# Attention and two gated feed-forward layers on one core: another layout of q and k in the attention's transposes and scores

## The chip, the cores and the metric

One core of a Trainium2 chip. The metric is the device time of one execution in microseconds; three runs of the kernel before gave 864.93, 865.22 and 866.91 us.

## What is computed

q, k and v have the shape (4, 8, 576, 64): batch, heads, tokens, head dimension; p has 32 rows per head instead of 576. All are float32.

```
def sm_attn(qq, kk, vv):
    s = scale * np.matmul(qq, kk.transpose(0, 1, 3, 2))
    s = s - np.max(s, axis=-1, keepdims=True)
    a = np.exp(s)
    a = a / (np.sum(a, axis=-1, keepdims=True) + 1e-09)
    return np.matmul(a, vv)
p_packed = sm_attn(p, k, v)
out = sm_attn(q, p_packed, p_packed)
x = out as 2304 tokens x 512
x = softplus(x @ w_in) @ w_out          # 512 -> 2048 -> 512
y = (sigmoid(x @ w_gate) * (x @ w_val)) @ w_out2    # 512 -> 1536 -> 512
```

## The kernel before

The work has three parts: the attention, the first feed-forward layer (lines 551 to 691) and the second (from line 701). The program is unrolled, and attention and first layer are woven into each other: `attn_unit` (line 380) is a generator, one unit is half of a batch's heads (4 heads, 8 units u = 0 to 7), and each `yield` ends a stage. `att_tick` (line 534) moves one unit on by a stage; the loop at line 880 calls it between the products of the first layer, through `between` (line 685), at a pace that has the units of a batch done when that batch's first layer begins. `jobs` holds the preparations of weights (three VectorE instructions per block of weight in `convert`, line 165). The order within each engine is then fixed when the program is built, by data readiness in a model of the engines; on the chip each engine takes its own queue in order.

Loads go out on SP's queue. `load_kqv` (line 218) reads a unit's k, q and v, each of 4 heads x 576 tokens x 64, into slots (areas of the tile `xa`, or the tile `acc6`), as 96 rows (partitions) of 6 tokens per head, 1,536 bytes in one piece. A slot is filled again when `done_kqv` has said that its last reader has been issued, and the transfer waits for that reader.

A unit's stages, as far as they matter here:

- p is transposed (line 384), and two ScalarE copies (line 387) put it in `pT`, a tile with zeros elsewhere, so that two heads stand in one product.
- `tr_pair` (line 357) turns k: for each pair of heads POOL copies the six chunks into the order chunk, head, dimension (`by_chunk`, line 348), TensorE transposes six blocks of 96x128 (line 362), and ScalarE evicts two banks of 288 columns (line 369). q goes the same way in later stages.
- Scores of p (line 400): four products of 288 columns over the full 128x128 array, two passes each, so eight instructions. Their 128 output rows are 4 heads x 32 rows of p, and each row has its 576 tokens in two banks (`s1`).
- The softmax over 576: maximum over both banks (line 408), one exponential with its sum (line 411), reciprocal, and the normalisation (line 420).
- The result a1 is transposed (line 434, evicted at line 435) and multiplied by v (line 453, 64 output columns in alternating halves of the array), which gives `pp`. Two ScalarE copies (line 463 calls line 96) put it in `bdT`, which the first layer's products of weights also read (lines 583 and 603). For units 0 to 2 `warm` (line 373) issues 12 instructions without a use of their result.
- Scores of q (line 478): 12 products, 24 instructions, of qT by `bdT`, and the softmax over 32 (lines 488 to 497; the last normalisation is POOL's), in two halves of 12x32 columns.
- Two stages later the result is transposed (line 506) and split into `A2h` and `A2l`, which the first layer reads (lines 113 to 115).

Lines 113 to 115 and 674 to 677 are the large products of the layers; line 587 and lines 610 to 620 handle the product of p's values and w_in.

## Time and profile before

| | us |
|---|---|
| median of three runs | 865.22 (864.93 to 866.91) |
| the profiled execution | 869.49 |
| its span in the trace | 867.7 |
| TensorE busy | 846.9 |
| VectorE busy | 587.9 |
| POOL busy | 475.8 |
| ScalarE busy | 339.8 |

The rows further down use short names: PE is TensorE's products and PEld its loads of the stationary side (beside PE), DVE VectorE, ACT ScalarE, POOL GpSimd, SP SyncE; a q behind a name is that engine's sequencer, and L362 is line 362 of the kernel before. An arrow <- names what is read, or what ended a wait. A line of code can be that of a helper that many call. Products are pipelined and the end of each is modelled, so distances between starts tell more than durations do. A granted clock of 1.00 is TensorE's full 2.4 GHz, 0.50 its lower level of 1.2 GHz.

### The profile page before, as it was taken

The numbers are of one execution on the slowest core, as the hardware profiler recorded it, in microseconds if no ns is written. First come the engines' busy times: TensorE is split into PE (matmuls) and PEld (weight loads), VectorE is DVE, ScalarE is ACT, GpSimd is POOL, SyncE is SP. The second block draws the span as 40 slices with busy tenths as digits, with TensorE's granted clock in tenths as the row PEclk, the third lists the DMA queues.
The fourth block names the chain that finished last, engine by engine and source line by source line (L and its number), as shares of the span: only waits on it lengthen the run. The fifth ranks groups of instructions, "written<-read, shape, count | busy, mean of one in ns | idle before, by whom it ended". The sixth has DMA issues, their size and how long they took to land.

```text
span 867.7 us, 15523 instructions
## 1 busy us (share of the span) xinstructions
PE 846.9 (98%) x6112; PEld 794.4 (92%) x6112; DVE 587.9 (68%) x1004; ACT 339.8 (39%) x626; POOL 475.8 (55%) x453
## 2 busy tenths in 40 slices
PE   7899999999999999999899999999999999999997
PEld 5789989999999999999889999999988999999996
DVE  1785566956365646646788687887897746667665
ACT  4367665554433434444433332222352432322210
POOL 4364333245655545575669786876984634436400
PEclk9899999999999999999999999999999999999999
DMA  9974321203033402400054655744515413213003
GB/s 227 209 207 117 83 56 29 74 25 99 1 98 92 135 12 87 127 26 1 1 177 146 188 152 149 207 132 128 163 51 151 115 47 90 67 43 110 13 1 109
DMA packets 58023, 85.53 MB, mean 99 GB/s; under 512 B 6368, under 2 KB 39264, under 8 KB 57952
## 3 DMA queue, kind: packets, MB, share of 16 engines
q1 hardware_dynamic: 56944, 83.31, 34.3%
q10 hardware_dynamic: 1008, 1.25, 0.4%
q8 instruction: 48, 0.79, 0.4%
q14 instruction: 23, 0.19, 0.1%
HBM read 65.67 MB, written 18.87 MB: 97 GB/s over the span
## 4 chain that ended last, share of the span: by engine, by line
PE 83%; DVE 8%; DMA 3%; ACT 2%; POOL 2%; issue 2%; SPq 0%; POOLq 0%; ACTq 0%; DVEq 0%
PE bank L115 8%; PE bank L113 8%; PE bank L114 8%; PE ps L674 7%; PE ps L675 7%; PE ps L677 7%; PE ps L1022 5%; PE ps L1023 5%; PE ps L1024 5%; PE ps L113 4%; PE ps L115 4%; PE ps L114 4%; PE ps L603 2%; PE ps L478 2%; PE ps L362 1%
## 5 line engine op out<-in xcount | busy, mean ns | idle before, releaser
L113 PE MATMUL bank<-aop,BH 128*128 128x288 f32 x672 | 199.2, 296 | 3.0 <-DVE work L987 1.1
L115 PE MATMUL bank<-aop,BL 128*128 128x288 f32 x672 | 198.9, 296 | 0.0
L114 PE MATMUL bank<-aop,BH 128*128 128x288 f32 x672 | 198.0, 295 | 0.2 <-DVE aop L101 0.2
L682 DVE TENSOR_TENSOR xa<-xa,ps 128x288 f32<-128x288 f32 x224 | 100.3, 451 | 105.8 <-PE ps L677 105.4
L101 POOL TENSOR_TENSOR ghl<-g,ghl 128x576 fp32r<-128x576 f32 x64 | 93.3, 1458 | 134.7 <-ACT ghl L108 125.2
L674 PE MATMUL ps<-ghl,woh 128*128 128x288 f32 x512 | 149.6, 307 | 2.6 <-DVE xa L682 2.4
L675 PE MATMUL ps<-ghl,wol 128*128 128x288 f32 x512 | 144.4, 297 | 0.0
L113 PEld LDWEIGHTS bank<-aop,BH 128*128 128x128 f32 x672 | 126.3, 188 | 8.7 <-issue 2.1
L114 PEld LDWEIGHTS bank<-aop,BH 128*128 128x128 f32 x672 | 126.6, 188 | 4.1 <-DVE aop L101 0.4
L115 PEld LDWEIGHTS bank<-aop,BL 128*128 128x128 f32 x672 | 126.6, 188 | 0.2 <-POOL BL L101 0.2
L101 POOL TENSOR_TENSOR BL<-cv,BH 128x512 fp32r<-128x512 f32 (+1 forms) x96 | 118.2, 1246 | 3.6 <-ACT BH L108 2.4
L677 PE MATMUL ps<-ghl,woh 128*128 128x288 f32 x512 | 109.5, 295 | 0.0
L674 PEld LDWEIGHTS ps<-ghl,woh 128*128 128x128 f32 x512 | 97.0, 189 | 5.1 <-ACT aop L737 2.1
L675 PEld LDWEIGHTS ps<-ghl,wol 128*128 128x128 f32 x512 | 97.2, 190 | 0.6
L975 DVE TENSOR_TENSOR work<-work,bank 128x576 f32<-128x576 f32 (+1 forms) x100 | 70.8, 724 | 30.7 <-PE bank L115 29.8
L1022 PE MATMUL ps<-oh,gv 128*128 128x512 f32 x216 | 84.5, 391 | 1.0 <-DVE xa L1030 0.5
L1023 PE MATMUL ps<-ol,gv 128*128 128x512 f32 x216 | 85.0, 393 | 0.0
L1024 PE MATMUL ps<-oh,gv 128*128 128x512 f32 x216 | 84.9, 394 | 0.0
L677 PEld LDWEIGHTS ps<-ghl,woh 128*128 128x128 f32 x512 | 82.7, 189 | 0.0
L1030 DVE TENSOR_TENSOR xa<-xa,ps 128x512 f32<-128x512 f32 x90 | 61.5, 684 | 28.8 <-PE ps L1024 28.4
L113 PE MATMUL ps<-A2h,wph 128*128 128x288 f32 x256 | 77.6, 303 | 0.3 <-ACT wph L587 0.3
L115 PE MATMUL ps<-A2h,wpl 128*128 128x288 f32 x256 | 76.3, 298 | 0.4 <-DVE wpl L101 0.4
(131 smaller groups left out, 1594.5 us busy)
## 6 DMA issues: line engine op xcount, KB each, us to landing
cv<-B SPq DMA_DIRECT2D x52, 256.0 KB, 2.7
B<-cv SPq DMA_DIRECT2D x48, 256.0 KB, 4.0
raw_in<-in_moe_w_in_dram SPq DMA_DIRECT2D x16, 512.0 KB, 3.9
raw_out<-in_moe_w_out_dram SPq DMA_DIRECT2D x16, 512.0 KB, 3.6
raw_g<-in_moe_w_gate_dram SPq DMA_DIRECT2D x12, 512.0 KB, 4.1
raw_v<-in_moe_w_val_dram SPq DMA_DIRECT2D x12, 512.0 KB, 4.5
raw_o<-in_moe_w_out_dram SPq DMA_DIRECT2D x12, 512.0 KB, 4.1
xa<-in_q_dram SPq DMA_DIRECT2D x6, 576.0 KB, 6.9
```

The lines of the kernel that those rows point to most:

```text
L101: eng.tensor_tensor(lo, x, hi.bitcast(F32), op=ALU.subtract)
L113: nc.tensor.matmul(ps, wh, xh, start=first, stop=False)
L114: nc.tensor.matmul(ps, wh, xl, start=False, stop=False)
L115: nc.tensor.matmul(ps, wl, xh, start=False, stop=last)
L674: nc.tensor.matmul(out_, wh[:, ms], gh[:, f], start=f == 0, stop=False)
L675: nc.tensor.matmul(out_, wl[:, ms], gh[:, f], start=False, stop=False)
L677: nc.tensor.matmul(out_, wo_hl[c, f][0][:, ms], gl[:, f], start=False, stop=f == 1)
L682: nc.vector.tensor_tensor(dst, dst, out_, op=ALU.add)
L975: nc.vector.tensor_tensor(to, x, y, op=ALU.add)
L1022: nc.tensor.matmul(bank, gh[:, ts_], oh, start=f == 0, stop=False)
L1023: nc.tensor.matmul(bank, gh[:, ts_], ol, start=False, stop=False)
L1024: nc.tensor.matmul(bank, gl[:, ts_], oh, start=False, stop=f == 1)
```

## The change

k and q are read as 128 rows, one for each of 4 heads x 32 groups of 18 tokens; a row is 4,608 bytes in one piece. Each block of 128 columns holds two neighbouring tokens, so a transposed block has the even token's 64 dimensions in partitions 0 to 63 and the odd one's in 64 to 127. `turn` makes three such transposes and one eviction, which puts the columns in the order that a1 and v need; POOL's copies by chunk are gone. v is read as before. k0 still comes in two transfers, cut by columns and no longer by heads.

The scores of p are, for each head, one product whose stationary side `pt_` holds p twice, once for each half, so that its 64 output rows are 2 parities x 32 rows of p; two heads fill the 128 rows of a bank, in alternating halves of the array. A row of p now has its 576 tokens in two rows of the same bank. The maximum of the two is found by a product with `swap` (which exchanges the halves) and a minimum of the negated values, their sum by a product with `both`. There is one exponential and one normalisation for each bank.

The scores of q read p's values from `bdq`, filled by four more copies (two on ScalarE, two on VectorE), and come in groups of 16x32 and 8x32 columns.

```
@@ load_kqv @@
             if tag == 6:
-                t = att.tile([CT, KQV], F32, tag="acc6", name=f"{nm}{u}")
+                t = att.tile([P, KQV], F32, tag="acc6", name=f"{nm}{u}")
             else:
-                t = xa[:CT, KQV * tag : KQV * (tag + 1)]
+                t = xa[:, KQV * tag : KQV * (tag + 1)]
             src = {"k": k, "q": q, "v": v}[nm][b, 4 * g : 4 * g + 4]
-            if nm == "v" and u >= VCH:
...
-            else:
-                t = t.rearrange("p (h c d) -> p h c d", h=4, c=NC)
-                n = 2 if (nm, u) == ("k", 0) else 4
-                for hh in range(0, 4, n):
-                    nc.sync.dma_start(
-                        t[:, hh : hh + n], src[hh : hh + n].rearrange("h (r c) d -> r h c d", c=NC)
-                    )
+            if nm == "v":
+                t = t[:CT].rearrange("p (h c d) -> p h c d", h=4, c=NC)
+                nc.sync.dma_start(t, src.rearrange("h (r c) d -> r h c d", c=NC))
+            else:
+                t = t[:, : 9 * P]
+                src = src.rearrange("h (r c) d -> (h r) (c d)", r=NK)
+                cut = 3 * P if (nm, u) == ("k", 0) else 0
+                for x in (slice(0, cut), slice(cut, 9 * P)):
+                    if x.start < x.stop:
+                        nc.sync.dma_start(t[:, x], src[:, x])
@@ constants @@
-    pT = [att.tile([P, 4 * P], F32, name=f"pT{i}") for i in range(2)]
-    for t in pT:
+    swap, both = (att.tile([P, 2, 2, NK], F32, name=y) for y in ("swap", "both"))
+    idv = ident.rearrange("p (e i n) -> p e i n", e=2, i=2)
+    for i in range(2):
+        nc.gpsimd.tensor_scalar(swap[:, :, i], idv[:, :, 1 - i], 1.0, 0.0, op0=ALU.mult, op1=ALU.add)
+    nc.gpsimd.tensor_tensor(both, swap, idv, op=ALU.add)
+    swap, both = (x.rearrange("p e i n -> p (e i n)") for x in (swap, both))
+
+    pT, bdq = (
+        [att.tile([P, 4, 2, NK], F32, name=f"{y}{i}") for i in range(2)] for y in ("pT", "bdq")
+    )
+    for t in pT + bdq:
         nc.gpsimd.memset(t, 0.0)
@@ by_chunk and tr_pair go, turn comes @@
+    def turn(src, n, dst):
+        ps = bank1()[:, : 3 * P]
+        for c in range(3):
+            o = (3 * n + c) * P
+            nc.tensor.transpose(ps[:, c * P : (c + 1) * P], src[:, o : o + P], ident)
+        nc.scalar.activation(
+            dst.rearrange("p h (m r x) -> p x m h r", m=3, x=3)[:, n],
+            ps.rearrange("p (m h r) -> p m h r", m=3, h=4), AF.Copy,
         )
@@ attn_unit @@
-        kT = att.tile([P, 2, S], F32, tag="kT", bufs=1, name="kT")
-        tr_pair(kt, 0, kT, nc.scalar)
-        yield
-        tr_pair(kt, 1, kT, E1)
+        kT = att.tile([P, 4, HS], F32, tag="kT", bufs=1, name="kT")
+        for n in range(3):
+            turn(kt, n, kT)
+            if n == 1:
+                yield
...
         s1 = bank2()
-        for hf in range(2):
-            for j in range(2):
+        for j in range(2):
+            for e in range(2):
                 nc.tensor.matmul(
-                    s1[:, hf, :HS],
-                    pT[u % 2][:, P * j : P * j + P],
-                    kT[:, j, hf * HS : (hf + 1) * HS],
-                    start=j == 0,
-                    stop=j == 1,
+                    s1[64 * e : 64 * e + 64, j, :HS],
+                    pt_[:, 2 * j + e].rearrange("p i n -> p (i n)"), kT[:, 2 * j + e],
+                    start=True, stop=True,
                 )
-        mx = att.tile([P, 4], F32, tag="mx", bufs=2, name="mx")
-        nc.vector.tensor_reduce(mx[:, 0:1], s1[:, :, :HS], op=ALU.max, axis=AX.XY)
...
+        mx = att.tile([P, 10], F32, tag="mx", bufs=2, name="mx")
+        nc.vector.tensor_reduce(mx[:, 0:2], s1[:, :, :HS], op=ALU.max, axis=AX.X)
+        nc.vector.tensor_scalar(mx[:, 2:4], mx[:, 0:2], -SC, None, op0=ALU.mult)
+        other = s1[:, 1, 508:510]
+        nc.tensor.matmul(other, swap, mx[:, 2:4], start=True, stop=True)
+        nc.vector.tensor_tensor(mx[:, 4:6], mx[:, 2:4], other, op=ALU.min)
+        a1 = att.tile([P, 2, HS], F32, tag="a1", bufs=1, name="a1")
+        for j in range(2):
+            nc.scalar.activation(
+                a1[:, j], s1[:, j, :HS], AF.Exp,
+                bias=mx[:, 4 + j : 5 + j], scale=SC, accum_out=mx[:, 6 + j : 7 + j],
+            )
+        total = s1[:, 1, 510:512]
+        nc.tensor.matmul(total, both, mx[:, 6:8], start=True, stop=True)
+        nc.vector.tensor_scalar(mx[:, 8:10], total, 1e-9, None, op0=ALU.add)
+        nc.vector.reciprocal(mx[:, 8:10], mx[:, 8:10])
+        for j in range(2):
+            nc.vector.tensor_scalar(
+                a1[:, j], a1[:, j], mx[:, 8 + j : 9 + j], None, op0=ALU.mult
+            )
...
         done_kqv("v", u)
         warm(u, pp[:, 3 * P :], 6)
+        for i in range(2):
+            for e in range(2):
+                copy(
+                    e == i, bq[64 * i : 64 * i + 64, e::2, i],
+                    heads(pp[64 * e : 64 * e + 64], 32 * e, 64),
+                )
...
-        for hf in range(2):
+        for ms in ((0, 1), (2,)):
             s2 = bank1()
-            for c in range(3):
+            w = 2 * P * len(ms)
+            for m in ms:
                 for j in range(2):
...
+                    for e in range(2):
+                        o = (m - ms[0]) * 2 * P + 64 * (odd ^ j) + 32 * e
+                        nc.tensor.matmul(
+                            s2[:CT].rearrange("p (c x) -> p c x", x=P)[
+                                :, 2 * (m - ms[0]) : 2 * (m - ms[0]) + 2, o % P : o % P + NK
+                            ],
+                            qT[:, 2 * j + e, m * CT : (m + 1) * CT],
+                            bq[:, 2 * j + e],
+                            start=True,
+                            stop=True,
+                        )
...
-            (nc.gpsimd if (u, hf) in PMU or u >= PMA else nc.vector).tensor_tensor(
-                a2, a2, m2[:, 1].unsqueeze(2).to_broadcast([CT, 12, NK]), op=ALU.mult
+            nc.gpsimd.tensor_tensor(
+                a2, a2, m2[:, 1].unsqueeze(2).to_broadcast([CT, n, NK]), op=ALU.mult
             )
```

## Rows read from the trace of the kernel before

**Rows 1.** The page, part 1: busy us (share of the span) xinstructions, TensorE's line.
```profile
PE 846.9 (98%) x6112; PEld 794.4 (92%) x6112; DVE 587.9 (68%) x1004; ACT 339.8 (39%) x626; POOL 475.8 (55%) x453
```
**Rows 2.** Windows: busy us (xinstructions) by engine, granted clock, DMA share, GB/s.
```profile
42.00:62.00 20.00, 19.04 (x190) 15.86 (x186) 18.06 (x33) 15.48 (x39) 11.78 (x11) 1.00 0.68 185
```
**Rows 3.** Waits of TensorE, 40 to 175 us: us in total, times, longest.
```profile
PE ps L506 <- POOL a L496: 1.0, 2, 0.7
```
**Rows 4.** Chain of waits at the start: start us, us, what.
```profile
6.26 10.95 DMA xa<-in_q_dram
...
17.39 0.84 POOL x L351
...
18.27 0.72 PE ps L362 x6
```
**Rows 5.** Windows before and in the fall of the granted clock.
```profile
16.50:18.50 2.00, 0.23 (x3) 0.23 (x4) 0.43 (x2) 0.48 (x2) 1.11 (x2) 1.00 1.11 229
18.50:25.50 7.00, 7.00 (x75) 6.71 (x74) 4.10 (x9) 2.88 (x8) 0.61 (x2) 0.56 0.97 252
```
**Rows 6.** Windows while q and v are read, and while a weight is read.
```profile
15.00:17.00 2.00, 1.48 (x11) 1.03 (x9) 0.94 (x3) 0.71 (x2) 0.00 (x0) 1.00 1.09 242
...
20.20:21.20 1.00, 1.00 (x14) 0.78 (x12) 0.00 (x0) 1.00 (x4) 0.00 (x0) 0.50 1.11 352
```
**Rows 7.** Chain of waits, steady part: TensorE's groups.
```profile
80.96 1.88 PE ps L583 x16
...
88.52 0.66 PE ps L434 x6
89.17 1.94 PE ps L400 x8
...
97.28 2.01 PE ps L478 x24
99.29 0.50 PE ps L362 x6
```
**Rows 8.** Timeline of TensorE after line 583: start us, us, what.
```profile
82.77 0.40 PE L113 MATMUL ps<-A2h,wph 128*128 128x288 f32 x1
83.01 0.29 PE L114 MATMUL ps<-A2l,wph 128*128 128x288 f32 x1
83.14 0.29 PE L674 MATMUL ps<-ghl,woh 128*128 128x288 f32 x1
```
**Rows 9.** Groups by line and form, 0 to 300 us: busy us, mean ns | idle before.
```profile
L351 POOL TENSOR_SCALAR x<-xa 96x768 f32<-96x768 f32 x22 | 19.2, 883 | 25.7 <-DMA xa<-in_k_dram 7.7 <-PE ps L362 5.9 <-issue 5.0
...
L369 ACT ACTIVATE kT<-ps 128x288 f32<-128x288 f32 x32 | 11.6, 409 | 4.7 <-PE ps L400 3.5 <-PE ps L362 0.6
...
L435 ACT ACTIVATE a1T<-ps 96x384 f32<-96x384 f32 x16 | 7.0, 483 | 0.7 <-PE ps L434 0.6
...
L185 DVE SCALAR_TENSOR_TENSOR w_in<-raw_in,w_in 128x512 int32<-128x512 int32 x6 | 5.7, 949 | 0.1
...
L96 ACT ACTIVATE bdT<-ps 64x64 f32<-64x64 f32 x16 | 3.5, 216 | 10.7 <-PE ps L378 7.1 <-PE ps L453 3.5
...
L411 ACT ACTIVATION_READ_ACCUMULATOR a<-ps,mx 128x1 f32 x8 | 1.6, 201 | 0.0
...
L409 DVE TENSOR_SCALAR mx<-mx 128x1 f32<-128x1 f32 x8 | 1.2, 144 | 0.1
```
**Rows 10.** One slot's way: timelines of SP, POOL, TensorE, and that load's landing.
```profile
114.59 0.31 SPq L237 DMA_DIRECT2D k<-in_k_dram  x1
...
113.73 0.83 POOL L351 TENSOR_SCALAR x<-q 96x768 f32<-96x768 f32 x1 [0.78 <-PE ps L362]
...
118.96 1.33 PE L362 MATMUL ps<-ident,x 96*128 96x96 f32 x12
...
121.97 0.73 PE L362 MATMUL ps<-ident,x 96*128 96x96 f32 x6
...
DMA to landing us min/median/max: 4.7/4.7/4.7
```

More of the change, by code (lines that the diff above doesn't have):

```diff
@@ L421, in attn_unit @@
+        for j in range(2):
+            nc.vector.tensor_scalar(
+                a1[:, j], a1[:, j], mx[:, 8 + j : 9 + j], None, op0=ALU.mult
+            )
         yield
         qt = kqv.pop(("q", u))
-        qT = att.tile([P, 2, S], F32, tag="qT", bufs=2, name="qT")
-        tr_pair(qt, 0, qT, nc.scalar)
-        yield
-        tr_pair(qt, 1, qT, E1)
+        qT = att.tile([P, 4, HS], F32, tag="qT", bufs=2, name="qT")
+        for n in range(3):
+            turn(qt, n, qT)
+            if n == 1:
+                yield
@@ L427, in attn_unit @@
         done_kqv("q", u)
         yield
-        a1T = att.tile([CT, NC, P], F32, tag="a1T", bufs=2, name="a1T")
-        for hf in range(2):
+        a1T = att.tile([CT, 2, 3, P], F32, tag="a1T", bufs=2, name="a1T")
+        for j in range(2):
             pa = bank1()
-            for c in range(3):
-                o = (3 * hf + c) * CT
-                nc.tensor.transpose(pa[:CT, c * P : (c + 1) * P], a1[:, o : o + CT], ident)
+            for m in range(3):
+                nc.tensor.transpose(
+                    pa[:CT, m * P : (m + 1) * P], a1[:, j, m * CT : (m + 1) * CT], ident
+                )
@@ L443, in attn_unit @@
             for c in range(NC):
-                if u >= VCH:
-                    nc.tensor.matmul(
-                        pp[:, 64 * j : 64 * j + 64],
-                        vt[:, c, 2 * j : 2 * j + 2].rearrange("p h d -> p (h d)"),
-                        a1T[:, c, 64 * j : 64 * j + 64], start=c == 0, stop=c == NC - 1,
-                    )
-                    continue
+                m, i = divmod(c, 2)
                 for e in range(2):
-                    n0 = 64 * j + 32 * e
+                    o = 64 * e + 32 * i
                     nc.tensor.matmul(
@@ L455, in attn_unit @@
                         vt[:, 2 * j + e, c, :],
-                        a1T[:, c, n0 : n0 + 32],
+                        a1T[:, j, m, o : o + 32],
                         start=c == 0,
@@ L461, in attn_unit @@
         warm(u, pp[:, 3 * P :], 6)
+        for i in range(2):
+            for e in range(2):
[3 more added lines that the diff above has]
+                )
         for e in range(2):
@@ L470, in attn_unit @@
         a2s = []
-        for hf in range(2):
+        for ms in ((0, 1), (2,)):
             s2 = bank1()
-            for c in range(3):
+            w = 2 * P * len(ms)
+            for m in ms:
                 for j in range(2):
-                    slot = odd ^ j
-                    o = c * P + 64 * slot
-                    t = (3 * hf + c) * CT
-                    nc.tensor.matmul(
-                        s2[:CT, o : o + 64],
-                        qT[:, j, t : t + CT],
-                        bdT[:, 4 * half + 2 * g + j, 64 * slot : 64 * slot + 64],
-                        start=True,
-                        stop=True,
-                    )
-            s2v = s2[:CT, : 3 * P].rearrange("p (x n) -> p x n", n=NK)
-            m2 = att.tile([CT, 2, 12], F32, tag="m2", bufs=4, name="m2")
-            a2 = att.tile([CT, 12, NK], F32, tag="a2", bufs=4, name="a2")
+                    for e in range(2):
[8 more added lines that the diff above has]
+                            stop=True,
+                        )
+            n = w // NK
+            s2v = s2[:CT, :w].rearrange("p (x n) -> p x n", n=NK)
+            m2 = att.tile([CT, 2, 16], F32, tag="m2", bufs=4, name="m2")[:, :, :n]
+            a2 = att.tile([CT, 16, NK], F32, tag="a2", bufs=4, name="a2")[:, :n]
             nc.vector.tensor_reduce(m2[:, 0], s2v, op=ALU.max, axis=AX.X)
             nc.vector.tensor_tensor(
-                a2, s2v, m2[:, 0].unsqueeze(2).to_broadcast([CT, 12, NK]), op=ALU.subtract
+                a2, s2v, m2[:, 0].unsqueeze(2).to_broadcast([CT, n, NK]), op=ALU.subtract
             )
@@ L495, in attn_unit @@
             nc.vector.reciprocal(m2[:, 1], m2[:, 1])
-            (nc.gpsimd if (u, hf) in PMU or u >= PMA else nc.vector).tensor_tensor(
-                a2, a2, m2[:, 1].unsqueeze(2).to_broadcast([CT, 12, NK]), op=ALU.mult
+            nc.gpsimd.tensor_tensor(
+                a2, a2, m2[:, 1].unsqueeze(2).to_broadcast([CT, n, NK]), op=ALU.mult
             )
-            a2s.append(a2.rearrange("p x n -> p (x n)"))
+            a2s += [a2.rearrange("p x n -> p (x n)")[:, o : o + P] for o in range(0, w, P)]
         yield
```

46 lines of the change are left out of this document (5 added, 41 removed).

## The prediction

> **What bounds the kernel now.** I read the page first: TensorE is busy for 98% of the span [rows 1], so time is won where TensorE has less to do, or where it stands still. The part under change is the attention, which ends near 157 us of the span. In windows of 20 us one stretch of it stands out, from 42 to 62 us, where another engine comes near the end of its time: VectorE works 18.06 of 20 us, TensorE 19.04 [rows 2]. The view of TensorE's waits says how little it stands there: from 40 to 175 us the largest entry is 1.0 us behind POOL's normalisation [rows 3]. So from 40 us on a change is worth what it takes from, or gives to, TensorE's own queue.
>
> The chain of waits shows the other place, the start. The load of unit 1's q is issued at 6.26 us and lands 10.95 us later; POOL then copies it by chunk (0.84 us), and TensorE's transposes of it begin at 18.27 us [rows 4]. From there to 32 us the chain is TensorE without a break. TensorE's clock belongs to this: in the 2 us before 18.5 the engine was busy for 0.23 us, and in the 7 us from 18.5 it had a granted clock of 0.56, mostly its lower level [rows 5].
>
> **The loads at the start.** Between 15 and 17 us the transfers are q and v, 96 rows each, and move 242 GB/s; around 20.7 us it is a weight of 128 rows, and they move 352 GB/s, both with the DMA share full [rows 6]. A k or q is 589,824 bytes: 2.44 us at the first rate, 1.68 at the second. With 128 rows of 4,608 bytes the second is the nearest row, so each load is 0.76 us shorter. Four of them (k0, k1, q0, q1) lie ahead of 18.27 us: -3.05 us. The POOL copy between landing and transposes goes too: 18.27 - 17.39 = 0.88 us [rows 4]. Together -3.9 us. Next late is unit 0's normalised a1, whose softmax gets longer (below); I take half a microsecond off for it: **-3.4 us**, ends 0 and -3.9. The number of issues on SP's queue is the same, in the same order. POOL's new start work (swap, both, four half-size memsets in place of two) lies beside loads that last to 17 us: nothing; without that cover it is under one POOL instruction of 0.83 us.
>
> **POOL.** Four copies a unit go, 883 ns each [rows 9], 28 us over eight units. POOL is not the bound, so only the 1.0 us that TensorE waited for a normalisation behind such copies can come back [rows 3]: -0.5 us, ends 0 and -1.0.
>
> **Transposes and their evictions.** Before: 24 transposes a unit of 96 columns, 6 in 0.50 us, 2.0 us. After: 18 of 128 columns, 6 in 0.66 us, 1.98 us [rows 7]: nothing. ScalarE evicted eight times 409 ns and now six times 384 columns, 483 ns by the row of that size [rows 9]: -0.37 us a unit. No row writes every third element; below I bound it by 409 ns, above by twice 483, 966, and take 483, the row of the same length. ScalarE has slack (15.48 of 20 us in rows 2), so this stays off the path.
>
> **Scores of p.** Now eight instructions of 288 columns over the full array, 1.94 us [rows 7]. After, the same eight with 64 output columns, alternating between the halves. The same form exists in this kernel: line 583 puts 64 columns in alternating halves, and 16 instructions of 256 columns take 1.88 us, 117 ns each, less than half of what the full form takes for its length [rows 7]. At 288 columns that is 132 ns, eight make 1.06 us: -0.88 us a unit. Units 0 and 1 make their scores while TensorE waits for loads; for the other six **-5.3 us**.
>
> **The two small products.** swap and both add four instructions a unit (two passes each), with a stationary side of 128 columns and 2 moving ones. No row has 2 columns. Line 478 loads 96 columns for 64 moving ones, 24 in 2.01 us, 84 ns each; the transposes of 128 columns take 110 ns [rows 7]. The ends are 0 (the loads hide under a neighbour) and 110; I take 110, as all 128 columns must be loaded: 0.44 us a unit, **+2.6 us** for six. The Trainium skill, TensorEngine Tiling (Array Packing), section Instruction Overhead, says that a matmul has some 60 cycles of overhead and that one of free size 1 lasts as long as one of 60. By that alone four would be an estimated 0.1 us a unit and the sum 2 us lower; the 84 ns of line 478 speaks against it. Besides, products of another kind start late: after line 583 the second product comes 0.24 us after the first, where 0.13 is usual [rows 8]. Each small product is an island of its own kind: two such gaps a unit, 0.22 us, **+1.3 us**, ends 0 and 2.6.
>
> **The waits that come with them.** TensorE takes its queue in order. The first product waits for VectorE's maximum, the second for ScalarE's two sums, and everything behind them on TensorE, the other stages' products too, waits along. The queue is built so that other products lie between; the waits that exist are small [rows 3]. Ends: 0, and one long VectorE instruction ahead, 0.95 us [rows 9], at each of 12 products, 11.4 us. I take 0.1 each, nearest to how the present waits come out: **+1.2 us**.
>
> **VectorE and ScalarE.** VectorE gets a minimum (144 ns), a second normalisation (about 0.1 more for the same elements) and two copies of 64x64 (about 0.2 each): 0.65 us a unit. ScalarE: the split exponential costs one more reading of the sum (201 ns) and some 0.1 of fixed cost, two more copies 216 ns each, less 0.37: +0.4 us [rows 9]. After 62 us TensorE's own queue covers this, as its short waits say [rows 3]. Between 42 and 62 us, with VectorE nearly full, two units add 1.3 us there [rows 2]; I take **+0.5 us** on the path, ends 0 and 1.3. The second softmax handles the same elements in pieces of 512 and 256; its scores keep their number and length: nothing.
>
> **Slots.** A k or q slot was free once POOL had copied it; now it is free when TensorE has transposed it. Unit 7's k is issued at 114.59 us, right after a copy begun at 113.73, while TensorE transposed that q from 118.96 us, and needed k at 121.97 [rows 10]. I take 0 here and price it as a rival.
>
> **Sum:** -3.4 - 0.5 - 5.3 + 2.6 + 1.3 + 1.2 + 0.5 = -3.6 us. The profiled execution took 869.49 us (span 867.7), so it would take 865.9; it stood 4.3 us above the median of the runs, 865.22, and I carry the difference over: **861.6 us**. By its ends this case runs from 859.5 to 864. A measurement of this kernel can tell about 0.3% from no change, 2.6 us: faster is below 862.6, slower above 867.8.
>
> **Rivals.**
> A, the clock does not fall. TensorE's queue before 18 us no longer holds the wait for the copies. Seven microseconds at 0.56 are 3.9 us of work at full clock: 3.1 us more are won, 858.5. For it: the fall followed 2 us with 0.23 us of work [rows 5]. Against it: q1's load still ends the wait, only earlier.
> B, the start does not get shorter: unit 0's softmax, with two products and a longer exponential in it, keeps the end of the wait where it was. Then -3.4 is missing: 865.0.
> C, slower: TensorE stands at the small products. VectorE's queue holds weight conversions of up to 0.95 us, and one of them stands ahead of the maximum's follow-up or of the minimum. At 0.65 us for each of 12 products it costs 7.8 instead of 1.2 us: 868.2. It decides from about 0.6 us a wait. For it: the chip's order of VectorE is fixed beforehand, and VectorE is nearly full from 42 us. Against it: the short waits now [rows 3].
> D, the slots. Transposed from 118.96 for 1.33 us, the q frees its slot at 120.3; less 3.4, 116.9. The load took 4.7 us and now 0.8 less: k would be there at 120.8, needed at 118.6, 2.2 us late. Two loads, k5 and k7, wait so: +4.4, 866.0. Against it: POOL's hop and copy also go.
> E, the halves do not run beside each other: the scores stay at 1.94 us, and the sum is 5.3 us higher, 866.9. The Trainium skill, TensorEngine Tiling (Array Packing), section Key Properties, says that tiles work independently but that a change of tiling mode drains the engine. Line 583 shows the gain net of any such drain [rows 7], so I hold E for unlikely.
>
> **How the numbers follow.** Chances: forecast 0.30, A 0.22, B 0.16, C 0.18, D 0.10, E 0.04. Faster: A, 0.25 of the forecast, 0.03 of B: 0.50. Slower: 0.17 of C, 0.02 of D, 0.01 of E: 0.20. The same: the rest, 0.30. The range reaches from 2 us under A, for its own unknowns, to C: 856.5 to 868.6; forecast, A, B, D and E lie in it, and half of C.
>
> **What would show it.** In the profile after: q1's transposes near 14.5 us; no POOL instruction in front of any transpose; the eight score instructions in about 1.1 us; the small products with short waits in TensorE's list; a granted clock from 14 to 25 us that tells A from the forecast. A start unchanged shows B, waits of the small products summing above 7 us show C, transposes waiting for DMA after 85 us show D, scores of 1.9 us show E. I am wrong if TensorE's work per unit rises, or if the loads of 128 rows move no more than 242 GB/s.

## The result, and the profile after

The kernel after took 877.85 us (median of 4 runs, 876.03 to 878.21) where the kernel before, run beside it, took 866.07: a ratio of 1.0124, with an interval of 1.0098 to 1.015. That is 11.8 us slower, and outside the forecast range. The profiled execution took 876.03 us, with a span of 874.3.

Part 1 of the page of the kernel after (busy us, share of the span, instructions):
```profile
PE 847.6 (97%) x6096; PEld 788.1 (90%) x6096; DVE 590.9 (68%) x1036; ACT 351.7 (40%) x642; POOL 449.7 (51%) x426
```
TensorE is busy for 0.7 us more than in [rows 1]: its work did not fall, though the scores of p take less (below). Without the small products it does fall, to 843.6 us (e7). ScalarE rose by 11.9 us, 1.5 a unit. POOL fell by 26.1. The span grew by 6.6 us, nearly all of it time in which TensorE stands.

Where it stands: five stretches of the attention, cut in both kernels at the same places of TensorE's work (6 us; the end of unit 1's products with v; the first product of the first layer's second weight, line 674 before and 675 after; the 37th, the 49th and the 109th product of that line). The windows of the kernel before (us, busy us of PE, PEld, DVE, ACT, POOL, then granted clock, DMA share, GB/s):
```profile
6.00:30.50 24.50, 20.29 (x212) 17.85 (x210) 9.04 (x21) 10.10 (x31) 6.75 (x9) 0.86 1.01 243
30.50:60.40 29.90, 26.78 (x258) 22.08 (x254) 24.88 (x53) 19.95 (x52) 16.48 (x16) 1.00 0.80 193
60.40:109.40 49.00, 48.52 (x499) 44.69 (x497) 28.83 (x72) 30.35 (x69) 21.11 (x22) 1.00 0.46 113
109.40:124.90 15.50, 15.50 (x122) 13.51 (x121) 9.57 (x25) 11.01 (x28) 7.76 (x8) 1.00 0.30 72
124.90:179.10 54.20, 53.63 (x489) 50.97 (x487) 40.49 (x84) 31.12 (x59) 15.40 (x13) 1.00 0.18 52
```
The same of the kernel after:
```profile
6.00:28.90 22.90, 19.37 (x208) 15.76 (x206) 9.62 (x26) 12.39 (x33) 0.00 (x0) 0.93 0.88 236
28.90:65.20 36.30, 29.99 (x253) 22.28 (x249) 26.82 (x64) 24.05 (x57) 11.77 (x9) 0.91 0.71 207
65.20:114.10 48.90, 48.19 (x495) 43.48 (x493) 30.05 (x80) 33.06 (x76) 11.84 (x12) 1.00 0.24 75
114.10:131.70 17.60, 15.40 (x119) 12.55 (x118) 9.49 (x27) 12.39 (x28) 4.38 (x4) 1.00 0.25 68
131.70:185.80 54.10, 53.92 (x486) 50.44 (x485) 40.17 (x90) 32.60 (x63) 13.98 (x11) 1.00 0.21 62
```
Length less TensorE's busy time is what it stands: before 4.2, 3.1, 0.5, 0 and 0.6 us, after 3.5, 6.3, 0.7, 2.2 and 0.2. Two stretches lost: the second by 3.2 us and the fourth by 2.2. Length times one less the granted clock is what the clock costs: before 3.4 us in the first stretch, after 1.6 and 3.3 in the first two. So over these stretches the profiles differ by 4.6 us of standing, 1.5 of clock and half a microsecond of work. The rest of the 11.8 us lies between profile and median: the profiled run of before, with a granted clock of 0.993, took 3.4 us more than the median shown here (of 63 runs of before whose clock is on record, 7 have 0.994 or less), and that of after was 1.8 us below its own. Over all their runs the granted clock averages 0.993 after and 0.997 before (the table below); of a span of 870 us that is an estimated 3.5. Over the whole spans TensorE stands 20.8 us before and 26.7 after (span less busy time). So about a third of the loss is clock and half of it, 5.9 us, is standing; the last 2.4 us these two profiles do not separate.

The start, in the chain of waits of the kernel after (start us, us, what):
```profile
5.65 10.71 DMA xa<-in_q_dram
16.36 0.14 issue
16.50 0.30 PE ps L358
```
and windows of its start and of the stretch behind it:
```profile
14.30:16.30 2.00, 0.00 (x0) 0.00 (x0) 0.33 (x1) 0.61 (x2) 0.00 (x0) 1.00 1.08 228
18.00:20.50 2.50, 2.50 (x20) 2.12 (x21) 0.20 (x2) 2.06 (x7) 0.00 (x0) 0.50 1.10 345
35.00:38.00 3.00, 1.65 (x12) 1.21 (x12) 2.23 (x6) 2.96 (x8) 1.15 (x1) 0.95 0.98 276
38.00:45.00 7.00, 6.91 (x27) 3.22 (x27) 3.26 (x13) 1.78 (x6) 1.62 (x2) 0.53 0.26 87
45.00:52.50 7.50, 5.37 (x41) 4.36 (x41) 5.25 (x14) 7.44 (x19) 1.77 (x1) 1.00 0.56 149
```
q1 lands at 16.36 us, 0.85 before [rows 4], and 0.61 of this is its earlier issue: while it is read, the loads move 228 GB/s, not the 352 of [rows 6]. TensorE's transposes of it start 1.77 us earlier than in [rows 4]: 0.92 because no copy stands between, 0.85 for the landing. Even this landing is luck: in the profiles of the eight kernels below that keep the order of these loads (e1 to e4, e7, e9, e12, e15) q1 lands between 16.67 and 18.43 us. TensorE stands for the 2 us ahead of them, and the clock falls to its lower level behind that (the second row), as in [rows 5]. It falls again from 38 us, behind a stretch of 3 us with 1.65 us of work.

TensorE's waits in the second stretch, 29 to 65 us, after (us in total, times, longest us):
```profile
PE ps L476 <- DVE bdq L98: 1.9, 2, 1.2
PE ps L393 <- ACT kT L359: 1.9, 2, 1.1
PE ps L358 <- ACT pT L379: 1.0, 1, 1.0
PE ps L431 <- ACT kT L359: 1.0, 2, 0.5
```
The chain of waits there shows why kT is late. It runs through ScalarE without a break until the scores of p begin (start us, us, what):
```profile
47.36 0.10 ACT pT L379
...
47.77 0.59 ACT woh L108
...
48.42 0.65 ACT t L651
49.07 0.58 ACT kT L359
49.66 0.49 ACT t L652
50.15 0.57 ACT kT L359
50.72 0.50 ACT t L653
51.21 0.57 ACT qT L359
51.79 0.52 ACT kT L359
52.31 0.04 issue
52.35 1.19 PE ps L393 x8
...
55.58 0.31 PE ps L402 x2
```
In the window from 45 to 52.5 us above, ScalarE is busy for 7.44 of 7.5 us. The kernel before has such a stretch too, with 7.05 of 7.5 us, and TensorE does not stand in it:
```profile
42.75:50.25 7.50, 7.50 (x57) 6.34 (x56) 6.62 (x12) 7.05 (x20) 5.50 (x5) 1.00 0.34 109
```
So a full ScalarE is not by itself what the change brought.

What ScalarE got, in its groups of the kernel after, 0 to 300 us (busy us, mean ns | idle before):
```profile
L359 ACT ACTIVATE qT<-ps 128x384 f32<-128x384 f32 x24 | 15.3, 687 | 3.9 <-PE ps L358 3.6
...
L406 ACT ACTIVATE a<-ps,mx 128x288 f32<-128x288 f32 x16 | 7.8, 496 | 3.0 <-DVE mx L403 2.8 <-PE ps L431 0.2
L379 ACT ACTIVATE pT<-ps 64x128 f32<-64x128 f32 x16 | 4.3, 270 | 6.4 <-PE ps L375 6.3
...
L96 ACT ACTIVATE bdq<-ps 64x64 f32<-64x64 f32 x16 | 3.5, 217 | 9.1 <-PE ps L369 3.9 <-PE ps L445 3.1 <-DVE bdq L98 2.0
```
An eviction takes 687 ns: six are 4.1 us a unit, where the eight of [rows 9] were 3.3. The fourth stretch holds three waits ahead of the transposes of unit 7's k, in TensorE's timeline after (what it waited for in brackets):
```profile
124.39 0.55 PE L358 MATMUL ps<-ident,q 128*128 128x128 f32 x3 [0.37 <-ACT qT L359]
...
126.99 0.87 PE L431 MATMUL ps<-ident,a 128*96 128x128 f32 x6 [1.03 <-DVE a L415]
...
128.66 0.87 PE L358 MATMUL ps<-ident,k 128*128 128x128 f32 x6 [0.69 <-DMA k<-in_k_dram]
```
SP issued the load at 124.97 us, when the q in its slot was transposed; in [rows 10] it had gone out at 114.59. Of the 2.2 us only 0.69 are the wait for k; 1.03 are a wait for VectorE's normalised a1 just ahead of it. Without the small products (e7 and e18 below) that one is gone, and the wait for k takes its place, 2.08 and 2.20 us; in e18:
```profile
124.37 1.51 PE L359 MATMUL ps<-ident,k 128*128 128x128 f32 x6 [2.20 <-DMA k<-in_k_dram]
```

### The profile page after: what moved, and what is told of

The parts are those of the page before. It is cut to its first block, busy times and chain, and to the rows that moved or that the text cites. A ratio compares the mean times of both kernels' runs of the same rounds, so it can differ in the third digit from the quotient of the medians.

```text
span 874.3 us, 15486 instructions
## 1 busy us (share of the span) xinstructions
PE 847.6 (97%) x6096; PEld 788.1 (90%) x6096; DVE 590.9 (68%) x1036; ACT 351.7 (40%) x642; POOL 449.7 (51%) x426
## 4 chain that ended last, share of the span: by engine, by line
PE 82%; DVE 8%; ACT 4%; DMA 3%; issue 2%; POOL 1%; SPq 0%; DVEq 0%; ACTq 0%; POOLq 0%
PE bank L115 9%; PE bank L113 9%; PE bank L114 9%; PE ps L675 7%; PE ps L676 7%; PE ps L678 7%; PE ps L1023 5%; PE ps L1025 5%; PE ps L1024 5%; PE ps L113 4%; PE ps L115 4%; PE ps L114 3%; PE ps L604 2%; PE ps L476 2%; PE ps L445 1%
## 5 line engine op out<-in xcount | busy, mean ns | idle before, releaser
L1005 ACT ACTIVATE work<-bank 128x576 f32<-128x576 f32 (+1 forms) x25 | 15.8, 633 | 152.2 <-DVE bank L976 152.2
```

## The experiments

Each line of the table is one kernel; "stands" is TensorE's standing time in its second stretch, from the end of unit 1's products with v to the first product of line 674, as above, in its one profiled execution; the clock is the mean of what its runs were granted. The medians are of 4 to 10 runs, which spread by 1.6 to 9.5 us, so that 2 or 3 us between two of them are not clear of noise. TensorE's order of work is that of after in e1, e5 and e9, and that of before in e6; in the others it came out changed in places when the program was built, so that they change more than their edit.

```
kernel                median us  ratio to before (interval)   clock  stands
before                  866.07                                0.997   3.1
after                   877.85   1.0124 (1.0098 to 1.0150)    0.993   6.3
e1_read                 875.60   1.0113 (1.0073 to 1.0153)    0.993   7.5
e2_flat                 874.90   1.0103 (1.0066 to 1.0139)    0.993   4.8
e3_bdq_act              877.99   1.0141 (1.0104 to 1.0178)    0.988   6.4
e4_slot                 881.15   1.0181 (1.0133 to 1.0228)    0.991   9.2
e5_q1_first             877.83   1.0128 (1.0088 to 1.0169)    0.989   5.6
e6_before_q1            865.90   0.9994 (0.9978 to 1.0010)    0.997   3.1
e7_no_exchange          873.52   1.0087 (1.0056 to 1.0118)    0.989   6.0
e8_mix                  872.22   1.0067 (1.0043 to 1.0090)    0.994   5.3
e9_bdq_blocks           877.32   1.0140 (1.0122 to 1.0157)    0.993   7.2
e10_mix_blocks          871.24   1.0061 (1.0039 to 1.0083)    0.996   6.3
e11_mix_slot            877.26   1.0139 (1.0120 to 1.0158)    0.988   6.2
e12_after_fill          882.83   1.0209 (1.0192 to 1.0226)    0.986   6.6
e13_mix_fill            873.80   1.0095 (1.0078 to 1.0111)    0.993   6.4
e14_before_fill         867.00   1.0014 (1.0001 to 1.0028)    0.997   2.6
e15_after_dve           881.73   1.0190 (1.0151 to 1.0230)    0.988   7.6
e16_mix_dve             877.74   1.0130 (1.0094 to 1.0166)    0.990   7.2
e17_mix_woh             877.53   1.0152 (1.0105 to 1.0200)    0.990   7.8
e18_mix_no_exchange     872.34   1.0075 (1.0047 to 1.0102)    0.990   6.3
```

**The evictions.** e1 lets each transpose take another block, so that the eviction reads PSUM in steps and writes neighbours; e2 writes the columns as they come, in another order of tokens.
```
-            o = (3 * n + c) * P
+            o = (3 * c + n) * P
...
-            dst.rearrange("p h (m r x) -> p x m h r", m=3, x=3)[:, n],
-            ps.rearrange("p (m h r) -> p m h r", m=3, h=4), AF.Copy,
+            dst.rearrange("p h (m r x) -> p m h r x", m=3, x=3)[:, n],
+            ps.rearrange("p (x h r) -> p h r x", x=3, h=4), AF.Copy,
```


> The changed kernel, but a bank now gathers the three blocks of one m, so that the eviction writes neighbouring elements and reads PSUM at a distance of 128 instead. If it is the writes at every third element that make an eviction last 687 ns, it comes down to about 483 ns (six per unit, -1.2 us of ScalarE a unit), the waits of TensorE for kT and pT between 30 and 53 us shrink, TensorE's clock no longer falls at 38 us (3.3 us), and the time falls by 4 to 7 us from 877.9 us. If a distance of 128 elements on PSUM's side costs as much as one of three on the other, it stays at 687 ns and 877.9 us. If the loss sits at the two small products, the copies into bdq or the slot of k, the time falls by less than 2 us although the eviction gets shorter.

> The changed kernel with evictions that read and write neighbouring elements only; the columns of kT and qT then stand in another order, so that scores of p are paired with the wrong rows of v. Work and waits are otherwise the same. Evictions of 483 ns and a time 4 to 7 us below 877.9 us if the strided writes are the cause; within 2 us of it if they are not. Against the run that gathers by m it separates PSUM's side from the other: equal times if reading at a distance is free.

ScalarE's groups of e1, 0 to 300 us:
```profile
L359 ACT ACTIVATE qT<-ps 128x384 f32<-128x384 f32 x24 | 11.1, 491 | 5.4 <-PE ps L358 5.1
L359 ACT ACTIVATE kT<-ps 128x384 f32<-128x384 f32 x24 | 11.0, 488 | 2.9 <-PE ps L393 1.4 <-PE ps L358 1.3
```
So the 200 ns were the writes at every third element; e2's evictions take 491 and 489 ns, so reading PSUM in steps costs nothing. In e1 that took 6.4 us from ScalarE's busy time (351.7 to 345.3). The medians fell by 2.3 and 3.0 us, less than the 4 to 7 expected and not clear of noise: the intervals of their ratios overlap that of after.

**The order of the loads.** e5 puts q1 ahead of v0 in the first loads of after, e6 in those of before.
```
-    PO = ['k0', 'k1', 'q0', 'v0', 'q1', 'v1']
+    PO = ['k0', 'k1', 'q0', 'q1', 'v0', 'v1']
```


> The changed kernel with the loads of the start in another order: unit 1's q ahead of unit 0's v. TensorE's one hole of 2.4 us and more ahead of unit 1's q (profiles: 2.4 to 3.1 us) and the fall of its granted clock that follows (1.7 to 6.8 us of clock lost before 33 us) should shrink if the landing of that q causes them: q lands about 2.5 us earlier, and the time falls by 3 to 6 us from 877.9 us. If the loss sits in the stretch from 29 to 65 us, where TensorE stood for 6.3 us in place of 3.1, the start only moves and the time falls by less than 2.5 us. If unit 0's v, now later, takes the place of the wait, it does not fall.

> The kernel before with the same other order of the loads at the start. There the wait for unit 1's q was 1.8 us and the clock fell for 7 us. If the landing of q decides in both kernels, it too falls by 2 to 5 us from 866 us; if only the changed kernel is held by it, it stays within 1.5 us.

Neither time moved: 877.83 and 865.90. The landing did. In e6 q1 is issued at 5.59 us and lands at 13.3, 3.9 us earlier than in [rows 4] and 3.1 earlier than in the profile of e14, which keeps before's order of loads:
```profile
L237 SPq DMA_DIRECT2D xa<-in_q_dram x1: 478/478/478, 5.6 to 5.6; - x1
...
DMA to landing us min/median/max: 7.7/7.7/7.7
```
In the seven kernels below that have this order with other edits (e8, e10, e11, e13, e16 to e18) it lands between 13.13 and 14.64 us. Only e5's own profile has 16.33; it is the slowest of that kernel's runs, and all its loads are late (v1 lands at 21.96 us, in after at 18.73). So e6 shows that an earlier q1 is worth nothing in the kernel before, to 0.2%; for the kernel after, e5 shows no gain in time, with a profile that does not have the earlier landing.

**The small products.** e7 leaves out the swap and both products, the minimum and the sum over partitions (the normaliser of each parity is its own).
```
-        nc.tensor.matmul(other, swap, mx[:, 2:4], start=True, stop=True)
-        nc.vector.tensor_tensor(mx[:, 4:6], mx[:, 2:4], other, op=ALU.min)
...
-        nc.tensor.matmul(total, both, mx[:, 6:8], start=True, stop=True)
-        nc.vector.tensor_scalar(mx[:, 8:10], total, 1e-9, None, op0=ALU.add)
+        nc.vector.tensor_scalar(mx[:, 8:10], mx[:, 6:8], 1e-9, None, op0=ALU.add)
```


> The changed kernel without the products with swap and both, the minimum and the sum over the halves: each parity of tokens is normalised by its own maximum and sum. It takes four instructions a unit from TensorE (about 0.6 us with the gaps around them, 4.7 us in all) and two trips through TensorE from each unit's softmax. If the longer chain of each unit is what makes TensorE stand between 29 and 65 us, idle time there goes from 6.3 towards 3.1 us and the time falls by 5 to 8 us from 877.9 us. If the small products cost only their own time, it falls by 2.5 to 4.7 us. If neither matters beside the clock, by less than 2 us.

873.52: without the exchange the time is 4.3 us shorter, and still 7.8 us longer than that of before run beside it (865.73). At like clock the exchange is worth more: three of e7's runs, granted 0.991, have spans of 871.0 to 871.5 us, and after's four, granted 0.992 to 0.994, have 874.3 to 876.5.

**The slot.** e4 gives unit 7's k a buffer of its own; e11 does the same on e10, below.
```
-        6: "565", 7: "656",
+        6: "565", 7: "756",
...
+            elif tag == 7:
+                t = att.tile([P, 9 * P], F32, tag="acc7", name=f"{nm}{u}")
```


> The changed kernel with a slot of its own for unit 7's k, which then need not wait for unit 6's q to be transposed. If the late slot costs what the profile shows between 124 and 129 us, the time falls by 2 us from 877.9 us and no transposes wait for DMA there. If TensorE would have waited for something else anyway, it stays within 0.7 us.

TensorE's waits of e4, 110 to 135 us, are now short:
```profile
PE ps L377 <- ACT qT L361: 0.4, 1, 0.4
...
```
The standing of the fourth stretch falls from 2.2 to 0.7 us, but that of the fifth rises from 0.2 to 1.7, 0.9 of it a wait for POOL, and the run is 3.3 us slower than after. TensorE's order of work changed with the slots, and the clock was low for 13 us early in its profile, behind 3 us without work:
```profile
14.80:17.90 3.10, 0.03 (x1) 0.00 (x0) 0.58 (x1) 0.86 (x2) 0.00 (x0) 0.89 1.08 212
17.90:31.00 13.10, 13.04 (x100) 12.19 (x101) 6.11 (x18) 5.67 (x15) 0.00 (x0) 0.51 0.66 197
```
So the slot's wait is shown, and what it is worth in time is not: part of it moved.

**The copies of the scores' matrix.** VectorE waits 5.6 us in all for ScalarE at bdq, as if the four copies stood in one chain. e3 puts all four on ScalarE (`e == i` becomes `True`); e9 lays the buffer out so that the copies touch separate blocks.
```
-        [att.tile([P, 4, 2, NK], F32, name=f"{y}{i}") for i in range(2)] for y in ("pT", "bdq")
+        [att.tile([P] + n + [2, NK], F32, name=f"{y}{i}") for i in range(2)]
+        for y, n in (("pT", [4]), ("bdq", [2, 2]))
...
-                    e == i, bq[64 * i : 64 * i + 64, e::2, i],
+                    e == i, bq[64 * i : 64 * i + 64, e, :, i],
...
```


> The changed kernel with all four copies into bdq on ScalarE instead of two on VectorE. If VectorE's weight conversions ahead of these copies cost time (2.4 us of waits in the profile, and the clock that falls after the second), the time falls by 2 to 4 us from 877.9 us. If ScalarE's queue is what is short, 0.44 us more on it per unit makes it 1 to 3 us slower.

> The kernel after with the buffer bdq laid out parity by parity, so that the four copies that fill it touch blocks that lie apart (e, j, i, n in place of 2j+e, i, n); the values are the same. In the profile of after the four copies, two on ScalarE and two on VectorE, follow each other in one chain (VectorE's wait 5.6 us in all for ScalarE's), and the products of the scores of q wait 2.4 us for them. If the series comes from the interleaved blocks and is a cause of the loss: VectorE's wait for ScalarE at bdq goes to under 1 us, TensorE's to under 1 us, its idle time between 29 and 65 us (6.3 us in after) falls to 4 to 5, and the time from 877.9 to 875 to 876.5. If the wait is only where slack shows (ScalarE's copies of pT and kT are late anyhow): the copies no longer wait for each other, TensorE waits as long for ScalarE elsewhere, 877 to 879.

Both stayed at after's time, and in e9 the wait is 5.6 us as in after: the blocks' layout is not what chains the copies. That theory falls.

**Taken together.** e8 has e1's evictions, q1 ahead of v0, and the sums' matrix bdT made by POOL from bdq, which takes two copies a unit from ScalarE; e10 adds e9's layout.
```
-            copy(
-                BDA, heads(to, 512 * half + 256 * g + 64 * odd + 32 * e, 64 if odd else 192),
-                heads(pp[r], 32 * e, 64),
+            nc.gpsimd.tensor_scalar(
+                heads(to, 512 * half + 256 * g + 64 * odd + 32 * e, 64 if odd else 192),
+                bq[r, e::2, e], 1.0, 0.0, op0=ALU.mult, op1=ALU.add,
```


> The changed kernel with three things together: evictions that gather by m (491 ns), unit 1's q ahead of unit 0's v, and the two copies into bdT made by POOL from bdq instead of by ScalarE from PSUM, which takes 0.43 us a unit from ScalarE. If the early stretch is bound by chains through ScalarE and VectorE, it falls by 5 to 9 us from 877.9 us, to about 871; to get below 866 us it would also need the start to hold no fall of the clock. If the gains are of the same waits, it is no better than the best of its parts.

> e8_mix (evictions with contiguous writes, q1 ahead of v0, the sums' matrix made on GpSimd) with the layout of bdq of e9. e8's waits of TensorE for VectorE's bdq were 4.4 us, the largest of all runs, so there is more to gain here: if the series is the cause, 872.2 falls to 868 to 870.5; with the slot's 2 us still there it doesn't reach the 865.7 of before. If the waits only move to another copy: 871.5 to 873.

> e10 with a slot of its own for the last block of k, as in e4. If the slot is worth the 2.1 us that TensorE idles between 124 and 129 us: 2 us below e10, 866 to 868.5, level with before. If the other order of work that comes with the slot gives it back, as e4 had it (a wait of the same size later): e10 or up to 3 us above it.

e8 won 5.6 us. e10 is the fastest of the kernels with the change, 871.24 us, 5.9 over the 865.3 of before run beside it; it is 1.0 below e8, which is not clear of noise, and e9 has shown that little of that is the layout's. e11 is 6.0 above e10, with a granted clock of 0.988 in place of 0.996; at like clock the two are level (e10's one run at 0.988 has a span of 875.0 us, e11's three at 0.988 and 0.989 have 874.0 to 876.3).

**The fillers.** Both kernels keep TensorE busy in units 0 to 2 with six products of the identity, in the bank that the copies then read, and the row of bdq above says that ScalarE waits 3.9 us for them (L369). e12, e13 and e14 put them into the next bank, in after, e10 and before.
```
-        warm(u, pp[:, 3 * P :], 6)
...
             s2 = bank1()
+            if ms[0] == 0:
+                warm(u, s2[:, :P], 6)
```


> The kernel after, with the six filler products of units 0 to 2 moved: they stood behind the products with v and wrote into the same PSUM bank, at columns that nobody reads; now they stand ahead of the scores of q and write into the bank of these scores, which overwrite them. In after's profile ScalarE's first copy of bdq waits 3.9 us in all for these fillers (three units) and TensorE then waits 2.4 us for the copies. If the copies are late because they wait for the fillers: both waits fall below 1 us, TensorE's idle time between 6 and 65 us (9.8 us in after) falls by 2 to 3, and the time from 877.9 to 873.5 to 876; where a fall of the clock followed from these stops, by up to 3 us more. If the copies are late because of their own series of four (e9 left that as it was): ScalarE's wait for the fillers goes, and TensorE waits as before; 877 to 879.

> e10 with the fillers moved in the same way. e10's waits of TensorE for bdq are 4.2 us between 6 and 66 us. If the fillers are the cause: 871.2 falls by 3 to 5, to 866 to 868.5, which is level with before but for the slot. If not: 870.5 to 872.5.

> The kernel before with the fillers moved in the same way. In its profile ScalarE's copies of bdT wait 7.1 us for the fillers, and TensorE 1.6 us for the copies. If a stop behind the fillers costs this kernel too: 865.7 falls to 863 to 865. If its two copies are short enough to hide, or the fillers only move: 865 to 866.5. Slower by over 1 us would mean that the fillers now delay the scores of q themselves.

TensorE's waits of e12, 29 to 69 us:
```profile
PE ps L508 <- POOL a L498: 2.1, 1, 2.1
PE ps L477 <- DVE bdq L98: 1.5, 1, 1.5
PE ps L393 <- ACT kT L359: 1.1, 1, 1.1
PE ps L431 <- ACT kT L359: 1.0, 2, 0.5
```
e12 is 5 us slower than after, e13 2.6 slower than e10, and e14 1.3 slower than before, with an interval just above 1. In e12 the waits for bdq and kT shrank a little (1.9 and 2.9 us in after), and a wait of 2.1 us for POOL's normalised a stands in their place: 6.6 us of standing, as after. Its clock was the lowest of all.

**ScalarE's load.** e15 and e16 move the third eviction of each kT and qT of units 0 to 3 to VectorE, in after and in e10; e17 moves four conversions woh from ScalarE to POOL in e10.
```
-        nc.scalar.activation(
+        copy(
+            not (n == 2 and early),
```


> The kernel after with the third of the three evictions of each kT and qT of units 0 to 3 on VectorE in place of ScalarE (8 evictions). In after's chain of work from 28 to 53 us ScalarE holds the end twice: 34.17 to 38.05 and 47.36 to 52.31 us, evictions of kT and qT between conversions; in the stretch 45 to 52.5 us it is busy for 7.44 of 7.5 us (before: 4.92), VectorE for 5.25. If ScalarE's load in this stretch is what TensorE waits for: a third of the evictions gone takes 2 x 0.69 us off that stretch, TensorE's idle time between 29 and 65 us falls from 6.3 to 4 to 5 us, and the time from 877.9 to 874.5 to 876.5. If VectorE is as full or the wait moves on, as in e9 and e12: 877 to 879.5; over 880 if VectorE's conversions fall behind.

> e10 with the same eight evictions on VectorE. They are contiguous there and take ScalarE 0.49 us each; ScalarE is busy for 7.44 of 7.5 us between 45 and 52.5 us here too, VectorE for 6.84. If ScalarE is the bound: 871.2 falls by 1 to 2.5, to 868.5 to 870; if VectorE (6.84 of 7.5) is next: 871 to 873.5.

> e10 with the first four conversions woh (0.63 us each on ScalarE, in the stretch up to 60 us) on GpSimd, which is busy for only 8.4 of 25 us between 28 and 53 us (before: 13.2, since it no longer sorts the blocks of k and q). If ScalarE is the bound of the stretch and the free GpSimd can take its load: 871.2 falls by 1 to 2, to 869 to 870.3. If not: 870.5 to 872.5.

e16 and e17 came out above every case, e15 at its last one, with VectorE busy for 2.4 us more in the second stretch than in after. That stretch of e15, and of e17:
```profile
35.30:71.90 36.60, 29.05 (x255) 22.90 (x251) 29.26 (x67) 21.48 (x54) 11.24 (x9) 0.95 0.60 185
```
```profile
27.00:64.70 37.70, 29.89 (x255) 23.52 (x251) 28.99 (x65) 20.23 (x51) 16.33 (x18) 0.91 0.69 210
```
ScalarE has 2.6 and 3.8 us less to do than in after's second stretch (most of the 3.8 is e10's, which has 20.6 us there), and TensorE stands 7.6 and 7.8 us, not less. ScalarE's load is where the chain runs; it is not by itself what holds TensorE.

**Two parts off at once.** e18 is e10 without the exchange of e7.

> e10 without the two small products, the minimum and the sum across partitions (the part that e7 leaves out: each parity of tokens is normalised by itself, which changes the result). e7 was 4.3 us below after, e10 6.6 us below it. If the two costs add, this run comes to 866 to 868: with cheap evictions and with the exchange for nothing, the change would be level with before, not faster, so the start and the early waits eat the products that it saves. Below 864: the exchange is the whole loss left, and a cheaper one would make the change pay. Above 869: the waits fill up again what the exchange leaves, as they did in e12 and e13.

872.34 is its last case: above e10, and only 1.2 below e7. In the medians the parts do not add. But e18's runs were granted 0.990 on average, e10's 0.996. At like clock the parts do add, nearly: e18's two runs at 0.986 have spans of 872.0 and 874.0 us, where e10's at 0.988 has 875.0; and its run at 0.993 has 867.4, where three runs of before at 0.993 have 866.5 to 867.7. So with e10's edits and without the exchange the change is about level with before at like clock, and most of the 7.1 us that it still loses is clock. What lowers its clock no edit shows; one fall in its profile, of 3.4 us from 124.2 us, comes right behind the wait for unit 7's k, which before does not have.

## Why the prediction was wrong

**The start, -3.4 us: the step that failed first.** It took the 352 GB/s of the weight in [rows 6] for the loads of 128 rows, and an earlier q1 for time won. Neither came. The kernel after moves 228 GB/s while q1 is read, under the 242 that the prediction itself named as a sign of being wrong, and q1's load takes 10.71 us against 10.95. And an earlier q1 wins nothing: e6 has it 3 to 4 us earlier and takes the time of before. In the profiles the copy came off, and q1's transposes start 1.77 us earlier; by the end of unit 1's products with v the two differ by 1.6 us, about what their clocks differ by. Rival B gave a start that wins nothing a sixth of the chance, for another reason (unit 0's softmax).

**Evictions at 483 ns, "off the path".** They took 687 ns, inside the bounds of 409 and 966, and the choice of the same-length row was wrong: the writes at every third element count. e1 and e2 put 2.3 to 3.0 us on it, not clear of noise.

**VectorE and ScalarE, +0.5 us: mis-sized most.** ScalarE was to get 0.4 us a unit more; the page has 1.5. Besides the evictions the sum left out that pT's copies are twice as wide (270 against the 218 ns that 64x64 copies take) and took 0.1 us for splitting the exponential, whose halves take 496 ns each where the whole took 744. It also priced the stretch before 62 us by engine shares over 20 us, [rows 2]. TensorE stands 3.2 us more there, and 3.3 us of clock come on top, in a fall that follows such a stop. That ScalarE's load is the reason is not shown: it lies on the chain, but before has 7.05 of 7.5 us of it without a stop, and e15 to e17 took load off it and won nothing.

**Scores of p, -5.3 us: right.** Eight take 1.19 us in the chain above and 1.12 later, predicted 1.06, before 1.94 [rows 7]. Rival E, that the halves would not run beside each other, is out.

**Small products, +2.6, +1.3 and +1.2 us: near in sum, not in its parts.** Predicted 5.1, e7 gives 4.3 in its median and somewhat more at like clock. The 110 ns were read off the wrong row: line 434 loads 96 columns and moves 128, and line 362, which loads 128, takes 83 ns [rows 7]. In after's trace the next product starts 0.14 to 0.56 us behind a small one (two passes of 2 columns), in seven of sixteen places 0.14; the last line of the chain above has 0.31, where 0.22 and a gap of 0.11 were taken. By the Trainium skill, TensorEngine Tiling (Array Packing), section Instruction Overhead, it would last as long as 60 columns, an estimated 0.05 us for two passes; the trace, with 0.14 us at the least, does not agree. TensorE's list of 29 to 65 us has no wait at them, so rival C, the one slower case, had the sign right and the place wrong. It is VectorE that waits at them, to 190 us:
```profile
DVE mx L412 <- PE ps L411: 10.1, 6, 3.3
DVE mx L403 <- PE ps L402: 6.7, 5, 2.8
```

**Slots, 0: wrong.** Rival D is right in its mechanism, and for k7 alone: TensorE waits 0.7 us for it in after, behind another wait, and 2.2 us, D's own figure, where the small products are left out (e18). k5 did not wait in after.

**POOL, -0.5 us: right.** To 190 us TensorE's list of the kernel after has no wait for POOL; before had 1.0 us of them [rows 3].

**The clock, rival A: wrong.** Without POOL's copy TensorE still stands for 2 us before q1, and the clock falls. Nor was there 3.1 us to win: the fall of [rows 5] belongs to a profiled run at 0.993, and the forecast had already gone down by 4.3 us to the median, where the runs at 0.997 and 0.998 lie.

**The working.** The case's range, 859.5 to 864, is not what its ends add up to: all the lower ends give 855.0, all the upper ones 877.8. That the time came out at the upper sum is luck: 11.4 us of that sum are waits of TensorE at the small products, of which its list shows none. And line 583's 117 ns are 54% of what the full form takes for that length, not under half; the sum used the 117 and is not touched by it.

What stays open: why the second stretch holds 4.8 to 9.2 us of standing in the profiles with the change and 2.6 to 3.1 in the three without it, and why the clock is lower with it. The evictions, the copies' engine and layout, the fillers, ScalarE's load and the exchange were each taken off, and the standing moved to another wait. That leaves the pace at which the stages of the units are called between the first layer's products, and the slots, both set for the old stages; another pace was not tried, and this is argued, not shown.

## What to carry to other kernels

A wait on the chain of one execution is not yet time to be won: move it alone first. Here a load that landed 3 to 4 us earlier won nothing in the kernel before. A change that exchanges one kind of product for another of equal cost is priced by the standing that it makes, which engine shares over tens of microseconds do not show. A bandwidth read in one stretch (352 GB/s, a weight) need not hold in another (228, q). And before two gains are said to add or not, compare runs at like granted clock: in the medians here 4.3 and 6.6 us did not add, at like clock they nearly did (e18).

## What the runs showed of the hardware

ScalarE's write of 384 float32 columns into SBUF at every third element takes 687 ns, 491 with neighbours; reading PSUM at a distance of 128 columns costs nothing beside it.

Loads of 128 rows were faster for a part of the start only: from 8 to 10 us, ahead of unit 0's q, the kernel after moves 294 GB/s and the kernel before, with 96 rows, 225; from 14 to 16 us, ahead of unit 1's q, it is 231 and 234. Why is not shown.

The runs of one kernel differ with the clock: e17's four runs had spans of 872.7 and 872.9 us at a granted clock of 0.996, 878.5 at 0.988 and 879.9 at 0.981; e10's had 867.6 to 869.6 at 0.998 and one of 875.0 at 0.988. In the profiles shown falls come behind a stop of TensorE, but not behind every one: e2's profile has a second stretch with 4.8 us of standing and a granted clock of 1.00:
```profile
27.00:62.00 35.00, 30.17 (x295) 23.43 (x296) 29.90 (x64) 21.95 (x56) 10.96 (x9) 1.00 0.72 221
```
In these two kernels 0.01 of clock goes with an estimated 4.7 and 6.4 us. Part of the differences between kernels in the table is therefore clock, and a stage with stops has to be compared at equal clock.
